# Four strided row loads for the query weights of a gated attention and MLP decode step

## The chip, the cores and the metric

The kernel runs on one core of a Trainium2 chip. The metric is the device time of one execution in microseconds; for the kernel before it is the median of three runs.

## The reference

Two branches read the same input `x` of 2 batch rows with 512 features, and a gate mixes them. The first is attention of one decode step over a cache, in a window of the last 4096 positions; the second is a dense layer, Mish, and a dense layer.

```python
def _A_ref(x, k_cache, v_cache, wq, wo):          # Hq, Dh = 32, 128; Hkv = 8
    W = min(4096, max(256, Sk // 4))
    q = (x @ wq).reshape(B, Sq, Hq, Dh).transpose(0, 2, 1, 3)
    k = jnp.repeat(k_cache[:, :, Sk - W:, :], rep, axis=1)
    v = jnp.repeat(v_cache[:, :, Sk - W:, :], rep, axis=1)
    p = _softmax(jnp.einsum("bhqd,bhkd->bhqk", q, k) * (Dh ** -0.5), axis=-1)
    o = jnp.einsum("bhqk,bhkd->bhqd", p, v)
    return o.transpose(0, 2, 1, 3).reshape(B, Sq, Hq * Dh) @ wo

def _B_ref(x, w1, b1, w2):
    h = jnp.einsum("bsd,df->bsf", x, w1) + b1
    sp = jnp.log1p(jnp.exp(-jnp.abs(h))) + jnp.where(h > 0, h, jnp.zeros_like(h))
    return jnp.einsum("bsf,fd->bsd", h * jnp.tanh(sp), w2)

g = _sigmoid((x * gate_w).sum(-1, keepdims=True))
return g * a + (1 - g) * b                        # a = _A_ref(...), b = _B_ref(...)
```

All data are float32: 8 MB of `wq`, 64 MB of keys and values in the window, 8 MB of `wo` and 7 MB of `w1` and `w2`.

## The kernel before

Weights and cache come from device memory into SBUF, the on-chip memory of 128 partitions, in large tiles of 128 partitions by 64 KB (`2 * CHUNK` float32 each). The pool `stream` has three such buffers, used in turn: first the query weights `wq`, then eight tiles `kv0` to `kv7` (one for each key/value head: transposed keys in the first half, values in the second), then `w12` (the first dense layer, the first rows of the output projection and of the second dense layer), then the remaining `wo`. A fourth tile takes over a buffer only when the work on its former tile is done.

All loads are issued by SyncE (SP) on one queue, in program order. `load` (L60) issues one DMA for each part of a tile; a part is a range of columns of all 128 partitions. The query weights come in two parts (L68): `wqh`, the first `HEAD` = 2048 columns, 1 MB, and `wqt`, the other 14336, 7 MB. Behind them on the queue stands the load of `sm` (L70), 13 KB with the input `x`, the gate's weights and a bias, and then the first key/value tiles.

Meanwhile GpSimd builds masks and zeroed tiles. When `sm` is there, it copies `x` into the padded tile `x32` (L92). `queries` (L123 to L140) runs twice, each time over half of the columns of `wq`: 64 small-output matmuls (L128, 32 columns of weights loaded, 512 columns moved), a scaled copy on ScalarE, four transposes on TensorE and two copies on VectorE into `qz`. Each matmul contracts over all 128 partitions of its columns.

For each key/value tile, `scores` (L144) does the matmuls with the keys, the row maxima and the exponentials; `turned` transposes these; `values` does the matmuls with the values. After the last tile come the dense layer (`hidden`), the output projection (L305) and the last sum (L315), and a store of the result.

Of the kernel before, what the change touches and what calls it, by code (L numbers as in the profile page):

```python
# [8 lines left out]
F32 = mybir.dt.float32  # L9
# [4 lines left out]
P = 128  # L14
# [18 lines left out]
FG = 4  # L33
HALF = 4
CHUNK = 8192
HEAD = 2048
SMALL = DC * B + DC + FC
SCALE = DH ** -0.5
CAP = 20.0
# [5 lines left out]


@with_exitstack
def decode_kernel(ctx: ExitStack, tc: tile.TileContext, res, stored, small, wqh, wqt, kv_in, w12, wo, w2, out):
    nc = tc.nc

    stream = ctx.enter_context(tc.tile_pool(name="stream", bufs=3))
# [6 lines left out]
    loads = []  # L58

    def load(name, *parts):  # L60
        t = stream.tile([P, 2 * CHUNK], F32, tag="s", name=name)
        x = 0
        for cols, src in parts:
            loads.append(nc.sync.dma_start(t[:, x : x + cols], src))  # L64
            x += cols
        return t

    wq_t = load("wq", (HEAD, wqh), (2 * CHUNK - HEAD, wqt))  # L68
    sm = const.tile([P, SMALL], F32, name="sm")
    loads.append(nc.sync.dma_start(sm, small))  # L70
    xT = sm[:, : DC * B].rearrange("p (c b) -> p c b", b=B)
# [337 lines left out]
```

## Time and profile before

| | us |
|---|---|
| median of 3 runs | 219.3 (219.29 to 219.37) |
| span of the profiled execution | 217.6 |
| busy, matmuls on TensorE | 113.0 |
| busy, VectorE | 21.5 |
| busy, ScalarE | 15.5 |
| busy, GpSimd | 8.0 |

The span goes from the first to the last instruction of one profiled execution; the time of a run also holds what lies around it. For the profiled execution itself only its span is recorded; the median of the runs is 1.7 us above it. The mean granted clock of TensorE was 0.867 of its full speed in it. A busy time is the sum over an engine's instructions, which overlap those of other engines, so the rows of the table do not add up to the span. Over the span the transfers moved 91.38 MB, a mean of 420 GB/s.

### The profile page before, as it was taken

How to read it: one execution, taken by the hardware profiler on the slowest of the kernel's cores; microseconds unless marked ns; L12 is line 12 of the kernel's file. 1: busy time of each engine (PE TensorE's matmuls, PEld its weight loads, DVE VectorE, ACT ScalarE, POOL GpSimd, SP SyncE). 2: the span in 40 equal slices, each digit the busy share in tenths (PEclk: the TensorE clock that was granted, in tenths of full speed). 3: DMA queues.
4: the chain of work that ended last, by engine and by line, in shares of the span. 5: the costliest groups of instructions: out<-in, count | busy, mean ns of one | idle time of the engine just before them, and what ended most of it. 6: DMA issues, size and time to landing. Idle time of an engine off the chain costs nothing.

```text
span 217.6 us, 1836 instructions
## 1 busy us (share of the span) xinstructions
PE 113.0 (52%) x822; PEld 33.8 (16%) x822; DVE 21.5 (10%) x32; ACT 15.5 (7%) x34; POOL 8.0 (4%) x30
## 2 busy tenths in 40 slices
PE   0000798477046608543660754286075418758596
PEld 0000322112011102101110210012011001214123
DVE  0000000010001230100123010010501001251000
ACT  2000001111001100200110020002002000301001
POOL 8000000000000000000000000000000000102100
PEclk9999999979658985995998599769759967999979
DMA  9797988898899889989998999899989999989892
GB/s 361 337 506 337 581 385 385 385 569 385 385 398 566 385 376 446 518 385 398 446 497 385 410 434 506 385 422 422 497 385 434 410 432 452 452 364 482 375 404 113
DMA packets 2550, 91.38 MB, mean 420 GB/s; under 512 B 416, under 2 KB 496, under 8 KB 752
## 3 DMA queue, kind: packets, MB, share of 16 engines
q1 hardware_dynamic: 2544, 91.28, 97.3%
q8 instruction: 6, 0.10, 0.2%
HBM read 91.24 MB, written 0.04 MB: 419 GB/s over the span
## 4 chain that ended last, share of the span: by engine, by line
DMA 77%; PE 18%; ACT 2%; DVE 1%; SPq 1%; issue 0%; ACTq 0%
DMA kv<-in_kv 61%; DMA wo<-in_wo 16%; PE sc L148 7%; PE o L172 5%; PE acc L305 4%; ACT p L153 1%; DVE mx L151 1%; PE pp L160 1%; PE fin L315 1%; ACT pT L161 1%; SPq L64 0%; SPq L70 0%; DVE res L348 0%; ACTq L161 0%; ACTq L153 0%
## 5 line engine op out<-in xcount | busy, mean ns | idle before, releaser
L148 PE MATMUL sc<-kv,qz 128*32 128x512 f32 x256 | 44.1, 851 | 54.1 <-DMA kv<-in_kv 54.1
L172 PE MATMUL o<-kv,pT 128*32 128x512 f32 x256 | 29.5, 596 | 5.8 <-ACT pT L161 5.8
L128 PE MATMUL qp<-wq,x 128*32 128x512 f32 x64 | 12.1, 799 | 23.0 <-POOL x L92 23.0
L148 PEld LDWEIGHTS sc<-kv,qz 128*32 128x32 f32 x256 | 9.9, 150 | 87.6 <-DMA kv<-in_kv 60.7
L151 DVE TENSOR_REDUCE mx<-sc 128x1 f32<-128x512 f32 x8 | 5.5, 691 | 112.4 <-PE sc L148 112.4
L153 ACT ACTIVATE p<-sc,mx 128x512 f32<-128x512 f32 x8 | 5.5, 687 | 131.2 <-DVE mx L151 131.2
L160 PE MATMUL pp<-ident,p 128*128 128x128 f32 x32 | 5.3, 287 | 12.1 <-ACT p L153 12.1
L172 PEld LDWEIGHTS o<-kv,pT 128*32 128x32 f32 x256 | 7.3, 109 | 20.9 <-issue 13.1
L305 PE MATMUL acc<-wo,padded 128*32 128x512 f32 x56 | 7.9, 728 | 2.2 <-DMA wo<-in_wo 2.2
L182 DVE TENSOR_REDUCE od<-om 128x256 f32<-128x1024 f32 x4 | 7.6, 1900 | 0.1
L128 PEld LDWEIGHTS qp<-wq,x 128*32 128x32 f32 x64 | 2.5, 137 | 28.9 <-POOL x L92 23.0
L179 DVE TENSOR_TENSOR om<-o,pick 128x1024 f32<-128x1024 f32 x4 | 4.9, 1225 | 19.3 <-PE o L172 19.3
L196 POOL TENSOR_TENSOR ms<-ms,top 8x64 f32<-8x64 f32 x2 | 0.6, 309 | 159.0 <-DVE top L194 159.0
L160 PEld LDWEIGHTS pp<-ident,p 128*128 128x128 f32 x32 | 3.4, 140 | 18.6 <-ACT p L153 18.6
L161 ACT COPY pT<-pp 128x512 f32<-128x512 f32 x8 | 4.7, 585 | 6.2 <-PE pp L160 6.2
L235 PE MATMUL hp<-w,x 128*32 128x512 f32 (+1 forms) x32 | 3.6, 543 | 2.3 <-DMA w<-in_w 2.3
L305 PEld LDWEIGHTS acc<-wo,padded 128*32 128x32 f32 x56 | 2.1, 129 | 8.0 <-issue 4.9
L305 PE MATMUL acc<-w,padded 128*32 128x512 f32 x22 | 2.8, 601 | 0.4 <-DVE padded L226 0.4
L117 DVE RECIPROCAL g<-g 128x2 f32<-128x2 f32 x1 | 0.2, 166 | 22.4 <-POOL g L116 22.4
L134 PE MATMUL qt<-ident,qs 128*128 128x128 f32 x8 | 1.3, 287 | 1.4 <-ACT qs L131 1.4
L112 PEld LDWEIGHTS zp<-xg,ones 128*128 128x128 f32 x8 | 1.8, 327 | 1.7 <-issue 1.7
L131 ACT ACTIVATE qs<-qp 128x512 f32<-128x512 f32 x2 | 1.2, 597 | 10.6 <-PE qp L128 10.6
(65 smaller groups left out, 31.3 us busy)
## 6 DMA issues: line engine op xcount, KB each, us to landing
wq<-in_wqt SPq DMA_DIRECT2D x1, 7168.0 KB, 21.4
w<-in_w SPq DMA_DIRECT2D x1, 6400.0 KB, 41.1
wo<-in_wo SPq DMA_DIRECT2D x1, 5120.0 KB, 34.8
wo<-in_wo SPq DMA_DIRECT2D x1, 2048.0 KB, 39.3
wq<-in_wqh SPq DMA_DIRECT2D x1, 1024.0 KB, 4.9
w<-in_w SPq DMA_DIRECT2D x1, 1024.0 KB, 41.3
w<-in_w SPq DMA_DIRECT2D x1, 512.0 KB, 42.0
w<-in_w SPq DMA_DIRECT2D x1, 256.0 KB, 42.1
```

The costliest lines, as they stand in the source:

```text
L128: nc.tensor.matmul(qp[Q * k : Q * k + Q, :], x32[:, c, :], w[:, c, k, :], start=(c == 0), stop=(c == DC - 1))
L148: nc.tensor.matmul(sc[Q * j : Q * j + Q, :], qz[:, kv, m * Q : m * Q + Q], t[:, (m * NJ + j) * 512 : (m * NJ + j + 1) * 512], start=(m == ...
L151: nc.vector.tensor_reduce(mx[:, kv : kv + 1], sc, axis=AX.X, op=ALU.max, negate=True)
L153: nc.scalar.activation(p, sc, AF.Exp, bias=mx[:, kv : kv + 1], accum_out=ls[:, kv : kv + 1])
L160: pin(nc.tensor.transpose(pp[:, c, :], p[:, c * P : (c + 1) * P], ident))
L161: nc.scalar.copy(pT, pp)
L172: pin(nc.tensor.matmul(o[Q * j : Q * j + Q], pT[:, c, Q * j : Q * j + Q], t[:, (c * NJ + j) * 512 : (c * NJ + j + 1) * 512], start=(c == 0 ...
L179: nc.vector.tensor_tensor(ov, pair[0].rearrange("p k (m d) -> p k m d", m=BN), pick[:, None, :, None].to_broadcast([P, 2, BN, DH]), op=ALU ...
L182: nc.vector.tensor_reduce(od[:, kv - 1 : kv + 1], ov.rearrange("p k m d -> p k d m"), axis=AX.X, op=ALU.add)
L235: nc.tensor.matmul(hp[Q * j : Q * j + Q, :n], x32[:, c, :], w[:, c, j * FG * P : j * FG * P + n], start=(c == 0), stop=(c == DC - 1))
L305: return nc.tensor.matmul(acc[Q * j : Q * j + Q, :], lhsT, rhs, start=(n_col[j] == 1), stop=(n_col[j] == n))
L315: nc.tensor.matmul(fin[Q * j : Q * j + Q, :], lhsT[:, y : y + Q], rhs[:, j * P : (j + 1) * P], start=(done[0] == 0), stop=(done[0] == n_fi ...
```

## The change

The tile of the query weights is no longer loaded by ranges of columns, but by sets of partitions, each with its full row of 64 KB. Four loads fill it: partitions 0, 8, 16, ... (16 rows, 1 MB); the odd ones (64 rows, 4 MB); 2, 6, 10, ... (32 rows, 2 MB); 4, 12, 20, ... (16 rows, 1 MB). In device memory `wqh` and `wqt` become one array `wq` of 128 rows of 64 KB, cut in the same way. Everything else stays.

```diff
-HEAD = 2048
+ROUNDS = (0, 8), (1, 2), (2, 4), (4, 8)
...
-def decode_kernel(ctx: ExitStack, tc: tile.TileContext, res, stored, small, wqh, wqt, kv_in, w12, wo, w2, out):
+def decode_kernel(ctx: ExitStack, tc: tile.TileContext, res, stored, small, wq, kv_in, w12, wo, w2, out):
...
-    wq_t = load("wq", (HEAD, wqh), (2 * CHUNK - HEAD, wqt))
+    wq_t = stream.tile([P, 2 * CHUNK], F32, tag="s", name="wq")
+    for a, step in ROUNDS:
+        loads.append(nc.sync.dma_start(wq_t[a::step], wq[a::step]))
...
-        "wqh": c(wq[:, :HEAD]),
-        "wqt": c(wq[:, HEAD:]),
+        "wq": c(wq),
```

## The prediction

> **What bounds the kernel now.** I read the page's DMA parts first, then its chain, then the stretches, then the first microseconds and the queries' stage in the timeline.
>
> ```profile
> span 217.6 us, 1836 instructions
> ...
> DMA  9797988898899889989998999899989999989892
> ...
> q1 hardware_dynamic: 2544, 91.28, 97.3%
> ...
> DMA 77%; PE 18%; ACT 2%; DVE 1%; SPq 1%; issue 0%; ACTq 0%
> ```
>
> The span's busy shares (tenths, in 40 slices) show the 16 DMA engines near full from the first slice to the last but one, and one queue's packets take 97.3% of 16 engines' whole span. The chain of waits agrees: 77% of it is transfers. The stretches say how steady this is:
>
> ```profile
> core 0: us, PE busy (x) PEld busy (x) DVE busy (x) ACT busy (x) POOL busy (x), PEclk, DMA share, GB/s
> 3.00:4.00 1.00, 0.00 (x0) 0.00 (x0) 0.00 (x0) 0.00 (x0) 1.00 (x1) 1.00 1.01 426
> ...
> 5.00:22.00 17.00, 0.00 (x0) 0.00 (x0) 0.00 (x0) 0.00 (x0) 0.06 (x1) 1.00 1.00 434
> ...
> 5.00:205.00 200.00, 103.34 (x702) 29.99 (x702) 21.02 (x30) 13.59 (x32) 3.67 (x16) 0.86 1.00 432
> ```
>
> The last two columns are the DMA share and the rate. From 5 to 205 us the stream never pauses: share 1.00, 432 GB/s. While the rest of the queries' weights come (5 to 22 us) it is 434, with the 8 KB rows before that 426. Sixteen engines at 434 are 27.1 GB/s each, whatever the row's length: a fixed rate of a lane. Everything ahead of the last matmuls hangs on this stream, so whatever delays or hastens its first 8 MB moves the end by the same amount, unless a later wait swallows it. TensorE does not: it is busy 103 of those 200 us.
>
> [...]
>
> **The change, part by part.** Four loads of 16, 64, 32 and 16 rows of 64 KB replace two of 128 rows (8 KB and 56 KB). The bytes are the same, the tile is the same, and the instruction order of the compute engines is unchanged; SP issues two more DMAs ahead of the small inputs' load.
>
> *Two more issues on SP.* The timeline prices them:
>
> ```profile
> 0.72 0.37 SPq L64 DMA_DIRECT2D wq<-in_wqh  x1
> ...
> 1.15 0.42 SPq L64 DMA_DIRECT2D wq<-in_wqt  x1
> ...
> 1.62 0.42 SPq L70 DMA_DIRECT2D sm<-in_small  x1
> ...
> 2.08 1.31 SPq L64 DMA_DIRECT2D kv<-in_kv  x2
> ```
>
> Two more at 0.42 us plus the 0.04 between them put the small load at about 2.5 us and the first two key/value loads at 3.0. Those wait behind the weights in the engines anyway, until some 22 us. Cost nothing; the cover is about 19 us deep. The first of the four loads carries 1 MB, 2.4 us of stream at 434 GB/s (1.049 MB / 434), so the second, issued 0.43 us behind it, is there in time.
>
> *The early head goes.* What did it buy?
>
> ```profile
> wq<-in_wqt SPq DMA_DIRECT2D x1, 7168.0 KB, 21.4
> ...
> wq<-in_wqh SPq DMA_DIRECT2D x1, 1024.0 KB, 4.9
> ...
> sm<-in_small SPq DMA_DIRECT2D x1, 13.0 KB, 21.1
> ```
> ```profile
> 22.76 0.20 POOL L92 COPY x<-sm 128x8 f32<-128x8 f32 x1 [17.70 <-DMA sm<-in_small]
> ...
> 23.01 1.91 PE L128 MATMUL qp<-wq,x 128*32 128x512 f32 x2 [23.01 <-POOL x L92]
> ...
> 38.16 0.33 SPq L64 DMA_DIRECT2D kv<-in_kv  x1
> ...
> 39.51 0.29 DVE L140 COPY qz<-qt 128x32 f32<-128x32 f32 x2 [4.66 <-PE qt L134]
> ...
> 42.01 4.48 PE L148 MATMUL sc<-kv,qz 128*32 128x512 f32 x24 [2.55 <-DMA kv<-in_kv]
> ```
>
> The head lands 4.9 us after its issue, at 5.6, but the first query matmul waits until 23.01 for x, which waits for the small load (1.62 + 21.1 = 22.7), which is queued behind all of the weights. So nobody uses the head early, and its loss costs nothing. The remainder of the stage moves with the stream: queries are done at 39.8, the first scores wait for key/value data until 42.0, and this margin of 2.2 us is kept since both ends hang on the same stream. The third key/value load is issued at 38.16, when a full load and more (19.3 us each) is still queued, so it does not come late either.
>
> *The start.* Windows count a packet where it starts:
>
> ```profile
> 1.70:1.85 0.15, 0.00 (x0) 0.00 (x0) 0.00 (x0) 0.15 (x1) 0.15 (x2) 1.00 3.09 437
> 1.85:2.30 0.45, 0.00 (x0) 0.00 (x0) 0.00 (x0) 0.14 (x1) 0.45 (x1) 1.00 0.00 0
> 2.30:2.50 0.20, 0.00 (x0) 0.00 (x0) 0.00 (x0) 0.00 (x0) 0.20 (x1) 1.00 0.41 82
> 2.50:2.75 0.25, 0.00 (x0) 0.00 (x0) 0.00 (x0) 0.00 (x0) 0.25 (x2) 1.00 0.87 295
> 2.75:3.00 0.25, 0.00 (x0) 0.00 (x0) 0.00 (x0) 0.00 (x0) 0.25 (x2) 1.00 0.96 360
> ```
>
> 437 GB/s over 0.15 us are 65.5 KB: exactly eight packets of 8 KB. Then none start for 0.45 us. Until 3.0 us the packets begun add up to 65.5 + 16.4 + 73.8 + 90 = 246 KB. [...] With 16 rows each engine has its row at once. The ends: nothing gained, or, if all ran at 434 from 1.70 on, (1.3 us x 434 - 246) / 434 = 0.73 us. Eight of 16 engines starting 0.8 us sooner are 0.4 us. But the early eight were slow too: none began a second packet before 2.3, though 8 KB at 27.1 GB/s are 0.3 us. I take **-0.2 us**, midway between nothing and 0.4.
>
> *Which engine writes where.* This is the term that decides. No row of this trace shows a load of fewer rows or of strided partitions; every weight and key/value load has all 128 in order. [...] A load of 16 rows must be dealt in another way. If that lets two engines write at once into partitions that share one entrance, each runs at half its 27.1 GB/s. The bounds: at full rate the 8.389 MB take 8.389 / 434 = 19.3 us as now, cost 0; with all pairs sharing all the time they take 38.7 us, cost **+19.3 us**. For the upper end speaks that the lane rate is so fixed (426 to 434 at any row length), which looks like a limit at the entrance, and that the engines, with equal rows in equal order, stay in step and so collide again at every row. I take the upper end, since that rate limit is the row nearest to it.
>
> [...]
>
> **Sum.** Profiled span 217.6 + 19.3 - 0.2 = 236.7 us. The median of the runs, 219.3, is 1.7 us above that span; I add the same: **238.4 us**. TensorE's closing work is unchanged and follows the last loads as before.
>
> **The rivals.**
>
> *No sharing: it does not matter where rows go.* Then only the start is left: 219.3 - 0.2 = **219.1 us**, from 218.6 (all of the 0.73) to 219.5. For it: the lane's 27.1 GB/s could as well be the engine's own limit, and a queue whose rows all sit on their own entrance (two rows for half of the engines first, the others soon after) would also lose nothing over the 8 MB. [...] This is the case on the other side: from a gain of over 0.44 us on, that is if at least 60% of the 0.73 is realised, it is faster than before.
>
> *Only the two loads of 16 rows collide.* If 64 and 32 rows are dealt by the same arrangement as 128, each engine keeps its own entrance there, and only 2 x 1.049 MB run at half rate: 2 x 2.42 = +4.8 us, **223.9 us**. [...] Against it: nothing shows that it scales with the number of rows or with a stride.
>
> *Pairs drift apart.* If one engine of a pair gets ahead by a full row, the two stop meeting at some rows. Some half of the loss is then saved: +8 to +14 us, **227 to 233 us**. For it: the engines start up to 1 us apart (1.70 to 2.75). Against it: with 16 rows they start together, and a shared entrance slows both equally.
>
> That the change does not do what it says can be left aside: the queue's order of issues has the four loads with 16, 64, 32 and 16 rows of 16384 elements in place of the two.
>
> **How the numbers follow.** All pairs share: 0.48. Drift: 0.10. Only the 16-row loads: 0.14. No sharing: 0.28. The likeliest gives 238.4 us, with a range of its own of 236 to 240: above for a shared entrance that loses a little in switching (5% of 38.7 us is 2), below for offsets between partners of up to one row (2.4 us). Without the last rival only 0.72 is held, so the range has to reach into it: **218.8 to 240.0 us**. About 0.2% (0.44 us) is what a measurement of this kernel tells from no change. Within the rival without sharing, a bit over a third is a gain beyond that, the rest is no change: faster 0.10, same 0.17, slower 0.73 (all cases of sharing, and 0.01 of the last).
>
> **What would show it.** Right: the queries' weights land at about 41 us and not at 22.6; the DMA share stays near 1.00 up to there, while the rate falls to about 217 GB/s; x is copied at 42, the first scores start at 61; from there all stretches are as before, 19 us later, at 432 GB/s. The two-halves start is gone: sixteen packets begin before 2.0 us. Wrong: if the weights land by 23 us, nothing is shared, and only the start is to be read; if they land at about 27, only the loads of 16 rows collided; between 30 and 37, partners drifted. If they land late and the end is not late by the same amount, the stream did not bound the kernel, and the first step fails. If the first scores wait for the queries and not for key/value data, the 2.2 us margin was used up.

## The result and the profile after

The changed kernel takes 224.74 us (median of 4 runs, 224.57 to 224.78) against 219.3 us (219.21 to 219.37): a ratio of 1.0244, 95% interval 1.023 to 1.0259. It is slower by 5.4 us; the forecast was 19.1 us slower. The profiled execution took 224.73 us with a span of 222.8 us (217.6 before). The measured time lies inside the range of 218.8 to 240.0 us, but only since that range had to reach down to the rival without sharing; the likeliest time, 238.4 us, is 13.7 us off.

From the page of the changed kernel, the lines that answer to those shown of before:

```profile
span 222.8 us, 1840 instructions
...
DMA  8989988988998998998998899899999898999993
GB/s 188 376 376 482 273 376 376 565 376 379 482 447 376 412 521 376 400 541 376 400 541 379 388 482 435 388 412 518 391 400 518 376 447 386 423 475 419 388 410 124
...
q1 hardware_dynamic: 2448, 91.28, 97.4%
...
DMA 75%; PE 19%; ACT 2%; SPq 1%; DVE 1%; issue 1%; ACTq 0%
```

The DMA share looks as full as before, and the queue's packets take 97.4% of 16 engines' span (97.3% before). The share does not show the loss (below, it is 1.00 at 204 GB/s as at 433); the rate does. The dip to 273 in the fifth slice (22.3 to 27.9 us, after 482 in the one before) is one place of it. Since a packet counts where it starts, and a row of 64 KB takes 2.42 us at the full rate (64 KB at the 27.1 GB/s of one engine), the slices are coarse; the stretches below are cut where one round of 16 packets ends and the next begins. In the first load 16 packets begin between 2.06 and 3.00 us and none from there to 6.70, so such a round is one row for each of the 16 engines. Last two columns: DMA share and GB/s.

```profile
core 0: us, PE busy (x) PEld busy (x) DVE busy (x) ACT busy (x) POOL busy (x), PEclk, DMA share, GB/s
2.05:6.70 4.65, 0.00 (x0) 0.00 (x0) 0.17 (x1) 0.00 (x0) 2.94 (x6) 1.00 1.07 226
6.70:9.85 3.15, 0.00 (x0) 0.00 (x0) 0.00 (x0) 0.00 (x0) 0.00 (x0) 1.00 0.93 333
9.85:21.95 12.10, 0.00 (x0) 0.00 (x0) 0.00 (x0) 0.00 (x0) 0.00 (x0) 1.00 1.00 433
21.95:26.55 4.60, 0.00 (x0) 0.00 (x0) 0.00 (x0) 0.00 (x0) 0.00 (x0) 1.00 1.04 228
26.55:29.60 3.05, 0.98 (x2) 0.18 (x2) 0.00 (x0) 0.00 (x0) 0.35 (x2) 1.00 0.97 348
30.00:205.00 175.00, 99.61 (x674) 28.64 (x673) 20.47 (x28) 13.60 (x32) 1.77 (x7) 0.84 1.00 432
```

The order of the loads can be read off: the first load of 16 rows at 226 GB/s, the odd partitions and every fourth from 2 at 433 (after a first round at 333), the last load of 16 rows at 228, and the first round of the first key/value tile at 348; from 30 us on 432, as before. So exactly the two loads of 16 rows run at about half rate. The round after each is slow too. It is counted together with them here: the round of 16 and the one behind it take 4.65 + 3.15 = 7.8 and 4.60 + 3.05 = 7.65 us together, where two rounds at 433 GB/s (1.049 MB each) take 4.84; the two pairs together lose 5.8 us, 0.7 us of it in the first pair being the slow start that a kernel without collisions has too (below, even and odd halves). That the second round is slow only because the engines leave the first at different times is not shown. The timeline of the queries' stage says where this arrives:

```profile
28.37 0.20 POOL L94 COPY x<-sm 128x8 f32<-128x8 f32 x1 [23.31 <-DMA sm<-in_small]
...
28.62 1.92 PE L130 MATMUL qp<-wq,x 128*32 128x512 f32 x2 [28.62 <-POOL x L94]
...
43.24 0.33 SPq L64 DMA_DIRECT2D kv<-in_kv  x1
...
44.59 0.29 DVE L142 COPY qz<-qt 128x32 f32<-128x32 f32 x2 [4.66 <-PE qt L136]
...
47.46 2.79 PE L150 MATMUL sc<-kv,qz 128*32 128x512 f32 x12 [2.90 <-DMA kv<-in_kv]
```

The query matmuls start at 28.62 (23.01 before), the first scores at 47.46 (42.01 before): 5.45 us late, which is the loss of the whole kernel (5.44). Nothing is given back and nothing added behind it, and the scores still wait for key/value data and not for the queries.

### The profile page after: what moved, and what is told of

It reads as the page before. It is cut to its first block, busy times and chain, and to the rows that moved or that the text cites. A ratio compares the mean times of both kernels' runs of the same rounds, so it can differ in the third digit from the quotient of the medians.

```text
span 222.8 us, 1840 instructions
## 1 busy us (share of the span) xinstructions
PE 114.2 (51%) x822; PEld 33.6 (15%) x822; DVE 21.5 (10%) x32; ACT 15.5 (7%) x34; POOL 8.0 (4%) x30
## 3 DMA queue, kind: packets, MB, share of 16 engines
q1 hardware_dynamic: 2448, 91.28, 97.4%
## 4 chain that ended last, share of the span: by engine, by line
DMA 75%; PE 19%; ACT 2%; SPq 1%; DVE 1%; issue 1%; ACTq 0%
DMA kv<-in_kv 61%; DMA wo<-in_wo 14%; PE sc L150 8%; PE o L174 6%; PE acc L307 3%; SPq L70 1%; ACT p L155 1%; DVE mx L153 1%; PE pp L162 1%; PE fin L317 1%; ACT pT L163 1%; SPq L72 0%; DVE res L350 0%; ACTq L163 0%; ACTq L155 0%
## 5 line engine op out<-in xcount | busy, mean ns | idle before, releaser
L174 PE MATMUL o<-kv,pT 128*32 128x512 f32 x256 | 30.9, 620 | 5.8 <-ACT pT L163 5.8
L130 PE MATMUL qp<-wq,x 128*32 128x512 f32 x64 | 11.5, 769 | 28.6 <-POOL x L94 28.6
L181 DVE TENSOR_TENSOR om<-o,pick 128x1024 f32<-128x1024 f32 x4 | 4.9, 1225 | 19.3 <-PE o L174 19.3
```

The lines of the kernel that those rows point to most:

```text
L130: nc.tensor.matmul(qp[Q * k : Q * k + Q, :], x32[:, c, :], w[:, c, k, :], start=(c == 0), stop=(c == DC - 1))
L174: pin(nc.tensor.matmul(o[Q * j : Q * j + Q], pT[:, c, Q * j : Q * j + Q], t[:, (c * NJ + j) * 512 : (c * NJ + j + 1) * 512], start=(c == 0 ...
L181: nc.vector.tensor_tensor(ov, pair[0].rearrange("p k (m d) -> p k m d", m=BN), pick[:, None, :, None].to_broadcast([P, 2, BN, DH]), op=ALU ...
```

## The experiments

Theories: **shared entrance**, engines writing at once into partitions that share one way into SBUF divide its rate; **memory side**, the reads of 16 engines at addresses 512 KB apart collide; **lone row**, an engine that has a single row in a load is slow, wherever it goes. An "entrance" is a name for this supposed shared way; no view shows one. "Collide" is said below of loads that come at a low rate, whatever lies behind it. That a set of partitions reaches a half or a quarter of the entrances is an assumption of the expectations below; the runs show rates alone. Unless said otherwise, the edit is to the changed kernel.

**Padded rows (e1_pitch).**

```diff
-        loads.append(nc.sync.dma_start(wq_t[a::step], wq[a::step]))
+        loads.append(nc.sync.dma_start(wq_t[a::step], wq[a::step, : 2 * CHUNK]))
...
-        "wq": c(wq),
+        "wq": c(np.pad(wq, ((0, 0), (0, 1024)))),
```

> The four loads of the change, but each row of the query weights in device memory is followed by 4 KB of padding (pitch 68 KB, not 64). Shared entrance (engines with one row each write in pairs through one SBUF entrance in the two loads of 16 rows): memory addresses play no part, 224.7 us, the 16-row loads again at about 211 to 220 GB/s. Memory side (in a load of 16 rows the 16 engines read at addresses 512 KB apart, which collide in the memory): the pitch is broken, the two loads run at 434 GB/s, 219.9 us. Lone row (an engine with one row in a load cannot overlap anything): 224.7 us.

Measured: 224.69 us (one run). The stretches of its two loads of 16 rows:

```profile
2.05:6.70 4.65, 0.00 (x0) 0.00 (x0) 0.17 (x1) 0.00 (x0) 2.93 (x6) 1.00 1.09 240
...
21.85:26.50 4.65, 0.00 (x0) 0.00 (x0) 0.00 (x0) 0.00 (x0) 0.00 (x0) 1.00 1.04 226
```

(The 240 of the first counts a seventeenth packet that began just before 6.70; 16 packets would be 226.) Addresses 544 KB apart are as slow as 512, so reads 512 KB apart are not the cause.

**Neighbouring halves (e2_halves).**

```diff
-ROUNDS = (0, 8), (1, 2), (2, 4), (4, 8)
+ROUNDS = (0, 64), (64, 128)
...
-    for a, step in ROUNDS:
-        loads.append(nc.sync.dma_start(wq_t[a::step], wq[a::step]))
+    for a, b in ROUNDS:
+        loads.append(nc.sync.dma_start(wq_t[a:b], wq[a:b]))
```

> Two loads of 64 neighbouring partitions, 0 to 63 and 64 to 127, rows of 64 KB. Shared entrance: each load reaches half of the entrances only, both run at half rate, 219.3 + 19.3 = 238.6 us, whichever engine has which row. Lone row: each engine has four rows in each load, full rate, 219.0 to 219.8 us. Memory side: no reading at 512 KB, 219.0 to 219.8 us. If the engines follow the partitions (one engine always the same entrance) the early half of the engines would start alone and the others catch up later: about 219.3 + 9.7 us at most if the second load queues strictly behind the first, no loss if not.

Measured: 240.73 us (one run).

```profile
6.80:22.19 15.39, 0.00 (x0) 0.00 (x0) 0.00 (x0) 0.00 (x0) 0.00 (x0) 1.00 1.00 204
27.10:42.55 15.45, 0.00 (x0) 0.00 (x0) 0.00 (x0) 0.00 (x0) 0.00 (x0) 1.00 1.00 204
45.60:205.00 159.40, 92.87 (x588) 25.24 (x586) 14.91 (x18) 10.92 (x24) 0.42 (x2) 0.81 1.00 434
```

No stride, four rows for each engine in each load on average, and both loads at 204 GB/s, less than half of 434, with a share of 1.00. So the set of partitions alone does it, and a load of 64 rows can collide throughout. By itself this does not say that the loads of 16 rows have the same cause.

**All rows at once (e3_whole)** and **even and odd halves (e4_evenodd).** One of the two new lines stands in each:

```diff
-ROUNDS = (0, 8), (1, 2), (2, 4), (4, 8)
+ROUNDS = ((0, 1),)             # e3_whole
+ROUNDS = (0, 2), (1, 2)        # e4_evenodd
```

> One load of all 128 partitions with 64 KB rows, no head, no strides. All theories: no collision. Prices the head alone: the eight late engines still start some 0.8 us behind the others, as before; 219.0 to 219.5 us.

> Two loads of 64 rows: the even partitions, then the odd ones. Shared entrance, with 64 rows dealt so that each engine keeps an entrance: no collision, 219.0 to 219.7 us (start a little earlier for the late engines, the strided issue some 0.2 us longer on SyncE). If the slow 7 to 10 us of the changed kernel belong to the strided load of 64 rows itself and not to the end of the first load, 219.3 + 0.6 us or more. Lone row and memory side: the same 219.0 to 219.7 us.

Measured: 219.6 us for the whole (ratio to before 1.0014, 1.0004 to 1.0024), 219.78 us for the halves (1.0021, 1.0012 to 1.0031). The first microseconds and the rest of the weights, first of the whole, then of the halves:

```profile
1.70:1.85 0.15, 0.00 (x0) 0.00 (x0) 0.00 (x0) 0.15 (x1) 0.15 (x2) 1.00 6.71 2185
1.85:2.30 0.45, 0.00 (x0) 0.00 (x0) 0.00 (x0) 0.15 (x1) 0.45 (x1) 1.00 4.36 1456
```
```profile
1.70:1.85 0.15, 0.00 (x0) 0.00 (x0) 0.00 (x0) 0.15 (x1) 0.15 (x2) 1.00 0.00 0
...
2.00:5.10 3.10, 0.00 (x0) 0.00 (x0) 0.17 (x1) 0.00 (x0) 3.00 (x6) 1.00 1.03 338
5.10:22.10 17.00, 0.00 (x0) 0.00 (x0) 0.00 (x0) 0.00 (x0) 0.00 (x0) 1.00 1.00 432
```

Two strided loads of 64 rows run at 432 GB/s from their second round on; the same number of rows side by side ran at 204. The changed kernel is 4.96 us behind these halves. If both pay the same for their start, that is the price of its two loads of 16 rows, 2.48 us each. The halves' first packets come late: none before 1.85. In the whole, 2185 GB/s over 0.15 us are 328 KB, five packets of 64 KB, and 1456 over 0.45 are 655 KB, ten more: 15 of 16 engines have begun by 2.30, as none of these packets can end within 0.6 us (2.42 at the full rate).

**Three loads without a lone row (e5_repaired).**

```diff
-ROUNDS = (0, 8), (1, 2), (2, 4), (4, 8)
+ROUNDS = (0, 4), (1, 2), (2, 4)
```

> Three loads: every fourth partition (32 rows), the odd ones (64), every fourth from 2 (32). Shared entrance: 32 and 64 rows were dealt without collision in the changed kernel (434 GB/s from 10 to 22 us there), so nothing collides here: 219.6 to 220.1 us, like the even and odd halves (219.78). Lone row: no engine has a single row, 219.6 to 220.1 us as well. If the cost of the change lay in the strides themselves or in the number of loads, about half of its 5.4 us or more would stay: 222 us and up.

Measured: 219.77 us (ratio 1.0011, 1.0 to 1.0021). Joining the two loads of 16 rows into one of 32 takes 4.97 of the 5.4 us away; the weights now come at the full rate:

```profile
5.00:22.05 17.05, 0.00 (x0) 0.00 (x0) 0.00 (x0) 0.00 (x0) 0.07 (x1) 1.00 0.99 431
```

**Eight loads of 16 strided rows (e6_eighths)** and **of 16 neighbours (e7_contig16).** The first is the change with

```diff
-ROUNDS = (0, 8), (1, 2), (2, 4), (4, 8)
+ROUNDS = (0, 8), (1, 8), (2, 8), (3, 8), (4, 8), (5, 8), (6, 8), (7, 8)
```

the second the neighbouring halves with

```diff
-ROUNDS = (0, 64), (64, 128)
+ROUNDS = tuple((x, x + 16) for x in range(0, 128, 16))
```

> Eight loads of 16 rows, every eighth partition from 0, 1, ... 7. Shared entrance: all eight run at half rate, 8 x 2.48 (half of the 4.96 us by which the change is behind the even and odd halves) = 19.8 above 219.78: 239.6 us. Drift (partners get out of step and stop meeting): 227 to 233 us. Lone row: 239.6 us too.

> Eight loads of 16 neighbouring partitions, 0 to 15, 16 to 31 and so on, one row for each engine as in the loads of 16 strided rows. Shared entrance: 16 neighbours reach a quarter of the entrances only, four engines on each, rate 434 / 4 = 108 GB/s: 8.389 MB take 77.3 us and not 19.3, 219.8 + 58.0 = 277.8 us. Lone row: it does not matter which partitions, half rate as with strides, 239.6 us.

Measured: 240.45 us and 274.67 us (one run each). From the second load on, first the strided, then the neighbours:

```profile
6.55:42.00 35.45, 0.00 (x0) 0.00 (x0) 0.00 (x0) 0.00 (x0) 0.00 (x0) 1.00 1.01 207
```
```profile
9.60:75.20 65.60, 0.00 (x0) 0.00 (x0) 0.00 (x0) 0.00 (x0) 0.00 (x0) 1.00 1.01 112
```

One row for each engine and load in both, and the rates are 207 and 112 GB/s: about a half and a quarter of 434. A lone row would not care which partitions, so that theory can't give the 112. Nor is it needed for the 207: the neighbouring halves, with four rows for each engine on average, lose the same (204). The 207 over the last seven loads also speaks against the drift, with which the kernel would have taken 227 to 233 us: the eight loads are 20.7 us behind the even and odd halves, 2.6 each. The 274.67 is 3 us under the 277.8 expected, as the rate is 112 and not 108.

A row's place in device memory follows its partition in all these loads, so both change together; only the padded rows moved one without the other. A further row speaks against the memory: the head of the kernel before is one contiguous piece of 1 MB, and so is each load of 16 neighbours. The head, spread over 128 partitions, came at 426 GB/s (3 to 4 us, in the prediction), the neighbours at 112.

**The head kept, the rest in halves (e8_head_evenodd).** An edit to the kernel before:

```diff
+ROUNDS = (0, 2), (1, 2)
...
-    wq_t = load("wq", (HEAD, wqh), (2 * CHUNK - HEAD, wqt))
+    wq_t = stream.tile([P, 2 * CHUNK], F32, tag="s", name="wq")
+    loads.append(nc.sync.dma_start(wq_t[:, :HEAD], wqh))
+    for a, step in ROUNDS:
+        loads.append(nc.sync.dma_start(wq_t[a::step, HEAD:], wqt[a::step]))
```

> The head of the kernel before (128 rows of 8 KB) first, then the other 7 MB as even and odd partitions. Asks what the even and odd halves alone (219.78, 0.4 to 0.5 us above before) lose. If it is the start (a first load of under 128 rows takes 0.55 us on SyncE instead of 0.37, and its first packets start at 2.05 instead of 1.72): the head starts as before, 219.2 to 219.5 us. If each strided load costs by itself: 219.7 us and up.

Measured: 219.47 us against 219.37 for the kernel before (ratio 1.0005, 0.9996 to 1.0014): no difference that can be told. The strided loads cost nothing that can be told by themselves behind a start as in before. The first microseconds of this run, whose first load is that of the kernel before:

```profile
1.70:1.85 0.15, 0.00 (x0) 0.00 (x0) 0.00 (x0) 0.15 (x1) 0.15 (x2) 1.00 3.91 437
1.85:2.30 0.45, 0.00 (x0) 0.00 (x0) 0.00 (x0) 0.15 (x1) 0.45 (x1) 1.00 1.03 146
```

The first stretch again holds eight packets of 8 KB, but here the second holds eight more (146 GB/s over 0.45 us are 66 KB), where the kernel before had none. The issue on SyncE of the first load, then that of the changed kernel's four (min/median/max in ns):

```profile
L70 SPq DMA_DIRECT2D wq<-in_wqh x1: 385/385/385, 0.7 to 0.7; - x1
```
```profile
L70 SPq DMA_DIRECT2D wq<-in_wq x4: 575/592/694, 0.7 to 2.6; - x4
```

**The same four loads in another order (e9_last).**

```diff
-ROUNDS = (0, 8), (1, 2), (2, 4), (4, 8)
+ROUNDS = (1, 2), (2, 4), (0, 8), (4, 8)
```

> The four loads of the change in another order: odd, every fourth from 2, every eighth from 0, every eighth from 4. Shared entrance: both loads of 16 rows collide wherever they stand, 224.5 to 225.0 us. If half of the loss belongs to the start (a slow first load), only one part is left: 222 to 223 us.

Measured: 224.82 us (ratio 1.025, 1.0235 to 1.0266). The loads of 64 and 32 rows, then the two of 16:

```profile
5.10:17.20 12.10, 0.00 (x0) 0.00 (x0) 0.00 (x0) 0.00 (x0) 0.00 (x0) 1.00 1.00 433
17.20:26.20 9.00, 0.00 (x0) 0.00 (x0) 0.00 (x0) 0.00 (x0) 0.00 (x0) 1.00 1.07 233
```

The slow rate moved with the loads of 16 rows, and the time did not change. They were slow in both orders.

No version tried beats the kernel before.

## Why the prediction was right and wrong

**What bounds the kernel: right.** The stream delays the first scores by 5.45 us and the end by 5.44. In the other kernels the first scores and the end move together as well. The farthest are the 16 neighbours: their first scores start 55.6 us late, and the kernel is 55.4 us late (274.67 against 219.3):

```profile
97.56 5.22 PE L150 MATMUL sc<-kv,qz 128*32 128x512 f32 x32 [2.93 <-DMA kv<-in_kv]
```

**The queue, the small load, the head's early matmul: right.** The queries again waited for x, and x for the small load behind all the weights. SyncE was slower than reckoned and issued the small load at 3.36 us and not at about 2.5, which cost nothing under that cover; the margin ahead of the first scores was kept, 2.6 us (47.46 - 44.59 - 0.29).

**The start: wrong in sign, small.** Forecast -0.2 us. What the new start costs is read from the loads without collisions, by their ratios to the kernel before: 0.5 us for the halves (1.0021), 0.2 us for the three loads (1.0011, an interval that begins at no change). That eight engines start 0.8 us sooner with a load of 16 rows, which gave the forecast's 0.4 us and so its -0.2, no run shows. The first packet comes later: between 2.06 and 2.10 in the changed kernel, and not before 1.85 in the halves, instead of 1.72. SyncE takes 0.55 to 0.73 us for each of these loads instead of 0.37 to 0.42. With the head in front no difference is left that can be told (219.47). Part of the cost is not settled: the whole in one load has an early start as well and is still 0.3 us over before, with an interval that begins at 0.04%.

Nor do eight early packets and a gap belong to a load of 128 rows. With 64 KB rows and the same 128 partitions (e3_whole), 15 engines begin by 2.30 without the gap. With the very load of the kernel before in front (e8_head_evenodd), sixteen packets begin by 2.30 and not eight. So the gap says nothing on how the rows of a load are dealt to engines. What it comes from stays open.

**Which engine writes where: the step that failed.** What stood: a load into some sets of partitions runs at a fraction of the rate (neighbouring halves 204 GB/s, 16 neighbours 112, 16 strided rows 207, with pitch and order ruled out). That engines share an entrance to SBUF there is the author's inference; no run shows it. The size of the upper end was right as well where all 8 MB collide: eight strided loads and neighbouring halves are 20.7 and 21.0 us behind the even and odd halves, against 19.3 in the prediction. What failed is the choice of the upper end, "all pairs sharing all the time", for the loads of 64 and 32 rows. These ran at 433 GB/s, so only 2 of the 8 MB collided: a term of +19.3 us that measured +4.96. The reason given for the upper end, that the lane rate is fixed and engines stay in step, fits the loads that collide (eight strided loads: 207 over the last seven), but says nothing on which loads do. How a load's rows are dealt to engines can't be seen in the profile; that in strided loads of 64 and 32 rows no two engines meet, as with 128, is inferred from their rate (433, against 434 with 128).

In its likeliest case the prediction took the four sets of partitions alike, as no view of before shows a load into fewer than 128. The runs tell them apart: the odd and the even partitions and every fourth one came at 431 to 433 GB/s, every eighth at 207, 64 neighbours at 204, 16 neighbours at 112. The number of rows does not decide (64 rows at 432 and at 204, 16 at 207 and at 112). Which partitions share what, and why every eighth is slow while every fourth is not, is not shown.

**The rival "only the two loads of 16 rows collide" is what happened.** It had 223.9 us and a chance of 0.14. Of the 0.84 us that it missed, by the even and odd halves 0.7 are the start (0.5 lost instead of 0.2 gained), and 0.1 is the price of the two slow loads, 2.48 us for each instead of 2.42. That its time came so close is in part that both errors were small; its condition, no collision in the loads of 64 and 32 rows, is what the rates show (433). The drift shows in no run.

## What to carry to other kernels

Where a load's rows go mattered here as much as how many there are: 16 rows at a stride of 8 partitions came at 207 GB/s, half the rate, and 16 neighbours at 112, about a quarter, while the odd ones or every fourth came at 431 to 433. So measure the rate of each part before a tile is split by partitions to start earlier. Here no such split gained: the kernels took 219.47 to 274.67 us against 219.3 to 219.4, and a split by columns over all 128 partitions (the kernel before) kept the quick issue (0.37 and 0.42 us) and the full rate (434). And a DMA share near 1.00 is not a full stream (it was 1.00 at 204 GB/s too): read the rate beside it, cut where rounds of packets end.

## What was not expected of the hardware

The loads at about half rate got less than half: 204 and 207 GB/s of 434, 5 to 6% under the half (the prediction's upper end of 240 us had allowed for 5%, an assumption of the author). The 16 neighbours got no less than a quarter (112, a quarter of 434 is 108.5).

And the issue of a load on SyncE differed with the set of partitions: 0.37 to 0.42 us for the query weights in 128 rows in order, 0.55 to 0.73 us for the strided loads of whole rows; in the two kernels with neighbours it was between 0.55 and 0.58 us for 64 rows, and 0.38 to 0.51 us for 16. The set is not all of it: the load of `sm`, 128 rows in order in every kernel, took 0.42 us before and 0.58 us right behind the strided loads of the change. What sets this time stays open.
